# Another list of attention steps in a fused attention and two-stage mixture-of-experts kernel

## The chip, the core and the metric

The kernel runs on one core of one Trainium2 chip. The time is device microseconds of one execution; three executions of the kernel before gave 986.51, 991.4 and 991.65 us, median 991.4. All other times here come from one profiled execution, whose own time is 991.88 us and whose span (first to last instruction) is 990.1 us.

## The reference, cut to what matters

Three layers follow each other. Attention with a block-causal mask works on 4 batches x 8 heads x 576 rows x 64 columns in f32; its output, as 2304 rows of 512, goes through a mixture of 8 experts with the two best experts of each row, and then through a second mixture with the one best expert of each row:

```python
scores = scale * np.matmul(q, k.transpose(0, 1, 3, 2))
scores = np.where(block_i >= block_j, scores, -1000000000.0)     # blocks of 64
attn = np.exp(scores - max) / (sum + 1e-09);  x = attn @ v
logits = x @ w_gate;  noisy = logits + log1p(exp(x @ w_noise)) * noise      # two best of 8
out[mask] += top2_w * (relu(x[mask] @ w1[e]) @ w2[e])
```

The second mixture has its own gate `w_gate2` (512 x 8) and its own weights.

## The kernel before, in words

Attention works on 16 pairs of heads. The work of a pair is cut into steps of two or three letters: TQ, TK and T4 transpose q, k and the last 64 rows on TensorE; QH, KH, A4 (ScalarE) and QL, KL, D4 (VectorE) split them into a high and a low part; S0, S1, S2, S8 are the score products; M and N the row maxima (VectorE), E the exponentials (ScalarE); B and BT transpose the exponentials, H and L split them; V0, V1, VX multiply with v, C copies, X0 and X1 multiply with an identity matrix beside the first gate's weights (IW), XC copies out.

TensorE, ScalarE and VectorE run in exactly the order in which the program issues the steps. That order is written out by hand in the string `ORDER` (lines 19 to 46 of the kernel), 1076 words. The n-th TK in it is that of pair n. Besides steps, there are three other words:

- `w3` puts three matmuls on a constant (L1161) into TensorE's queue.
- `a` takes one step of the routing of the first mixture.
- `h` takes the next entry of a list of side jobs ("heap") that is sorted by a time written beside each entry. There are 26 words `h`. The first four entries are `consts1` (small constants, eight noise loads nz, the triangle matrix tri on VectorE), `consts2` (more constants, the loads of wg2 = `w_gate2`, mid and bias1), the first part of `consts3`, and the load of the first quarter of expert weights; after them come zero fills of X1 and X2 in DRAM, three more quarters of weights and their splits.

```python
elif n == "h":
    heapq.heappop(heap)[2]()
...
for kk in range(4):
    ten.transpose(pt[:, kk], wg2[:, kk], ident)      # consts3, first part
act.activation(wt, pt.rearrange("e k d -> e (k d)"), AF.Copy)
```

So the first part of `consts3` puts four transposes of wg2 into TensorE's queue and a copy into ScalarE's, at the place of the third `h`.

GpSimd (POOL) and the queue that issues most loads and stores (SP) are not in the hand-written order; a scheduler places their instructions. Both still run one after the other: an instruction that waits holds all behind it. The loads of k and q for pair p+3 are issued when TQ, TK and T4 of pair p are; the step VS of pair p+2 (split of v on POOL) comes behind V0, V1 and VX of pair p, and the load of v for pair p+4 behind that. Lines: L906 and L911 are the loads of q, k, v; L200 and L201 the noise; L217 wg2; L218 mid; L226 the zero fills; L1147 and L1148 the stores of attention rows into X1; L472 the weights. L92 is a recording layer through which all compute instructions go.

After attention a part that is emitted by a clock model of the program runs both mixtures; nothing of it is touched.

Of the kernel before, what the change touches and what calls it, by code (L numbers as in the profile page):

```python
# [16 lines left out]
ET = mybir.EngineType  # L17

ORDER = """
TQ TK T4 h QH KH A4 h QL h KL w3 S1 h S2 TK TQ D4 M1 M2 E1 KH E2 QH T4 w1 S0 w2 S8 M0 KL M8 QL N8 A4 E0 w1 B5 w2 S1  # L20
B0 H5 E8 H0 D4 L5 M1 S2 B3 B2 E1 H3 H2 L0 M2 L3 L2 BT S8 VX B1 B4 HT E2 H1 H4 CX M8 LT N8 L1 L4 S0 TK TQ T4 V0 E8 KH
QH A4 C0 M0 KL QL h D4 R2 h BT S1 h V1 B3 B5 E0 HT H3 H5 M1 LT L3 L5 B0 S2 B2 B4 H0 C1 E1 H2 H4 L0 M2 L2 L4 VX h B1
h S0 TK TQ CX H1 E2 L1 M0 T4 V0 S8 KH QH A4 C0 E0 R2 KL D4 M8 QL N8 V1 S1 B0 h B1 X0 E8 H0 H1 C1 XC0 M1 L0 L1 S2 B3
B2 B4 E1 H3 H2 H4 M2 L3 L2 L4 S0 X1 B5 VX BT E2 XC1 H5 HT CX M0 L5 LT TK S8 V0 T4 TQ KH E0 C0 A4 QH KL M8 N8 R2 D4
QL B0 V1 B1 S2 X0 H0 H1 E8 C1 XC0 L0 L1 M2 BT B3 S1 X1 HT H3 E2 XC1 LT L3 R2 M1 B4 B2 S0 B5 VX H4 H2 E1 H5 CX L4 L2
L5 M0 X0 TQ h TK V0 S8 XC0 KH QH C0 E0 QL KL M8 N8 T4 B5 V1 S1 B0 A4 E8 C1 H5 H0 D4 M1 L5 L0 X1 S0 h BT B4 E1 XC1 HT
H4 M0 L4 LT B1 VX S2 B3 B2 H1 E0 H3 H2 CX L1 M2 L3 L2 X0 S8 TQ TK V0 E2 QH XC0 KH M8 N8 QL KL R2 C0 E8 h X1 T4 V1 B4
S1 A4 XC1 H4 C1 D4 h M1 L4 B3 B0 S2 BT H3 H0 HT E1 L3 L0 LT M2 B2 B1 VX B5 S0 H2 H1 CX H5 E2 L2 L1 L5 M0 TK TQ V0 T4
S8 KH QH C0 E0 A4 QL KL M8 D4 R2 N8 V1 B0 B5 h S1 B1 H0 C1 H5 H1 E8 L0 L5 L1 M1 X1 XC1 TQ VX B3 BT S0 QH H3 HT E1 QL
L3 LT R2 M0 X0 B4 B2 S2 CX XC0 H4 H2 E0 L4 L2 h M2 X0 TK V0 T4 S8 KH XC0 C0 E2 A4 M8 KL N8 D4 V1 B5 B0 B2 S8 H5 H0  # L30
H2 E8 C1 L5 L0 L2 M8 N8 X1 BT B3 S1 XC1 HT H3 E8 LT M1 L3 B1 VX B4 S0 H1 H4 CX E1 L1 L4 R2 M0 TK TQ V0 S2 T4 QH KH
C0 E0 A4 QL KL M2 D4 V1 BT B0 S0 TQ HT H0 C1 E2 QH LT L0 M0 QL R2 X0 XC0 X1 h S2 X1 X0 XC1 E0 XC1 XC0 B2 B1 B4 S1 H2
H1 M2 L2 L1 H4 L4 M1 TK E2 KH a B3 VX KL H3 L3 S8 E1 B5 a H5 M8 L5 h CX TQ a a N8 QH QL a E8 S2 TK KH V0 T4 C0 A4 a
M2 a BT S1 V1 R2 a KL a D4 a E2 B5 HT B3 M1 H5 S8 a LT a B0 h L5 B2 a H3 E1 L3 H0 S0 B4 a M8 a C1 L0 a H2 L2 B1 VX a
H4 L4 X0 a H1 CX L1 TQ XC0 a TK N8 QH E8 a M0 a V0 QL T4 S2 a KH C0 KL V1 B5 a A4 E0 D4 a H5 a M2 B1 S8 a a H1 L5 E2
a B0 L1 H0 a X0 C1 a h S0 a M8 a XC0 N8 L0 a E8 B4 R2 B3 B2 a H4 M0 a L4 a H3 L3 a VX S1 H2 E0 X1 BT HT L2 a T4 M1
S0 A4 a LT a D4 a CX M0 a a a V0 E1 XC1 C0 S8 B4 a a R2 E0 V1 B0 a M8 a a H4 H0 a N8 E8 a X0 L4 L0 S1 a XC0 B1 H1 a
TQ QH L1 BT QL HT a LT M1 C1 a S2 B2 TK H2 KH a L2 X1 a VX E1 KL B5 XC1 M2 a H5 L5 a X1 B3 a S1 E2 H3 L3 M1 a S0 XC1
T4 a TQ CX A4 E1 D4 a TK M0 V0 QH QL a C0 S8 a KH E0 B1 M8 KL V1 B3 a S2 H1 H3 B5 R2 L1 N8 H5 E8 C1 L3 L5 a X0 XC0 h
a B4 B0 S2 X1 a H4 a M2 H0 a L4 a E2 XC1 L0 B2 VX H2 M2 a BT T4 S0 CX HT L2 TK a h h LT V0 A4 a E2 D4 a TQ KH B5 a  # L40
M0 C0 QH a a S1 a KL QL a E0 a a V1 B0 a H5 B3 H0 a M1 S8 a a L5 H3 a X0 E1 L0 BT a M8 L3 R2 N8 a C1 S2 B4 XC0 a HT
LT E8 H4 M2 VX a B2 B1 L4 H2 L2 S0 CX a H1 L1 a X1 E2 a T4 a M0 a V0 A4 XC1 a C0 a a D4 E0 a a BT S1 V1 M1 a h B5 S8
a HT a LT a a E1 H5 a C1 a a B0 H0 a JT0 M8 JH0 L5 JT1 N8 X0 a JH1 L0 a h R2 X1 B1 XC0 a JL0 JL1 a E8 VX B2 H1 XC1 a
a a JM0 CX a B3 a H2 L1 R2 B4 JM1 a a a a L2 JR0 a H4 JV0 a JM2 L4 a a H3 L3 a V0 JS0 JR1 C0 JR2 JV1 JM3 B0 a a V1
B2 JM4 BT JM5 JV2 a JR3 JS1 H0 H2 HT JV3 a L0 L2 LT JR4 JR5 a JV4 JV5 a h a C1 a B5 a VX B3 B1 JM6 a H5 a L5 a B4
JM7 JS2 H3 CX H1 H4 JR6 a L3 a L1 L4 JR7 a JV6 a X1 JV7 V0 JS3 X0 XC1 a C0 V1 X0 XC0 C1 XC0 X1 a XC1
"""


# [1643 lines left out]
```

## Time and profile before

| | us |
|---|---|
| median of three executions | 991.4 |
| the profiled execution's own time | 991.88 |
| its span | 990.1 |
| TensorE busy | 925.7 |
| VectorE, GpSimd, ScalarE busy | 676.0, 506.9, 465.1 |

The page cuts the span into 40 slices of 24.75 us with the busy share of each engine in tenths. A view of stretches gives the busy time of each engine between two times. The timeline gives instructions with start, duration, names and, in square brackets, how long the engine had stood idle before and what ended that. The view of waits sums up these by engine and by what was waited for.

### The profile page before, as it was taken

Reading aid. Unit: us, or ns where it says so; the run is one execution under the profiler, and the core shown is the slowest. Engines: PE = TensorE matmul, PEld = TensorE weight load, DVE = VectorE, ACT = ScalarE, POOL = GpSimd, SP = SyncE. Lnnn points to the kernel's source line nnn. Section 1 sums busy time; section 2 is a strip of 40 time slices with the busy share of each in tenths; the row PEclk is TensorE's granted clock in tenths of the full one; section 3 lists DMA queues with packets and bytes.
Section 4 is the critical chain, followed back from the end, with each engine's and each line's share of the span. In section 5 each row is a group of like instructions: output and inputs, shape, how many; then the busy total and the mean of one; then the engine's idle time right before and its main releaser. Section 6 shows DMA issues by size and latency. Waiting matters only on the chain. (4 is left out here: it accounts for less than half of the span.)

```text
span 990.1 us, 16259 instructions
## 1 busy us (share of the span) xinstructions
PE 925.7 (93%) x5655; PEld 807.8 (82%) x5655; DVE 676.0 (68%) x1639; ACT 465.1 (47%) x1026; POOL 506.9 (51%) x585
## 2 busy tenths in 40 slices
PE   2599999999889988999999999999999999999995
PEld 1378888878879877998989899897988878888895
DVE  1497888988838789839487593979859686233241
ACT  1498989877644143433333333333333333343352
POOL 3044455385231665968486684847966226222122
PEclk7799999999999999999999999999999999999998
DMA  6784433223158545747365463734646446443440
GB/s 128 215 257 118 120 92 93 66 80 81 34 170 269 107 92 144 160 126 144 94 146 111 127 130 88 143 95 86 151 126 128 123 139 191 139 128 107 138 130 13
DMA packets 145292, 124.49 MB, mean 126 GB/s; under 512 B 75625, under 2 KB 115945, under 8 KB 145074
## 3 DMA queue, kind: packets, MB, share of 16 engines
q1 hardware_dynamic: 126242, 90.14, 31.4%
q0 software_dynamic: 17904, 32.96, 17.0%
q8 instruction: 47, 0.77, 0.3%
q10 hardware_dynamic: 1056, 0.26, 0.1%
q14 instruction: 43, 0.35, 0.1%
HBM read 95.50 MB, written 28.09 MB: 125 GB/s over the span
## 5 line engine op out<-in xcount | busy, mean ns | idle before, releaser
L92 POOL TENSOR_TENSOR wl<-raw,wh 128x1024 fp32r<-128x1024 f32 (+1 forms) x91 | 189.4, 2128 | 97.8 <-ACT wh L92 95.3
L92 DVE SCALAR_TENSOR_TENSOR zero<-py,gts,wide 128x512 f32<-128x512 f32 x296 | 221.6, 749 | 8.2
L92 PE MATMUL ph<-xth,wh 128*128 128x312 f32 (+4 forms) x672 | 217.1, 323 | 4.3 <-DVE kp L92 3.4
L92 PE MATMUL ph<-xtl,wh 128*128 128x312 f32 (+4 forms) x672 | 216.8, 323 | 0.4 <-DVE xtl L92 0.4
L92 PE MATMUL ph<-xth,wl 128*128 128x312 f32 (+4 forms) x672 | 217.0, 323 | 0.0
L92 PE MATMUL py<-wh,kp 128*128 128x512 f32 x488 | 165.2, 399 | 3.7 <-DVE zero L92 3.7
L92 PEld LDWEIGHTS ph<-xth,wh 128*128 128x128 f32 x672 | 127.6, 190 | 10.0 <-DVE kp L92 3.7
L92 PEld LDWEIGHTS ph<-xtl,wh 128*128 128x128 f32 x672 | 127.4, 190 | 5.8 <-DVE xtl L92 0.6
L92 PEld LDWEIGHTS ph<-xth,wl 128*128 128x128 f32 x672 | 127.0, 189 | 5.1
L92 ACT ACTIVATE wh<-raw 128x1024 fp32r<-128x1024 f32 x112 | 117.8, 1052 | 4.6 <-DMA raw<-in_moe_w_dram 4.6
L92 ACT ACTIVATE yr<-py,gts 128x512 f32<-128x512 f32 x59 | 40.6, 689 | 152.1 <-PE py L92 103.4
L92 PEld LDWEIGHTS py<-wh,kp 128*128 128x128 f32 x488 | 92.4, 189 | 23.3 <-DVE zero L92 4.4
L92 PE MATMUL py<-wl,kp 128*128 128x512 f32 x244 | 95.9, 393 | 0.0
L92 DVE SCALAR_TENSOR_TENSOR hl<-ph,hh 128x312 fp32r<-128x312 f32 (+5 forms) x84 | 43.0, 512 | 76.0 <-ACT hh L92 74.5
L92 PE MATMUL py<-wh,hh 128*128 128x512 f32 x228 | 92.8, 407 | 0.0
L92 PE MATMUL py<-wh,hl 128*128 128x512 f32 x228 | 89.7, 393 | 0.0
L92 PE MATMUL py<-wl,hh 128*128 128x512 f32 x228 | 89.5, 393 | 0.0
L92 POOL DMA_INDIRECT X<-yr,ids x40 | 63.4, 1585 | 44.6 <-ACT yr L92 25.8
L92 POOL DMA_INDIRECT xr<-X,ids x54 | 54.9, 1017 | 61.0 <-PE px L92 46.5
L92 ACT ACTIVATE hh<-ph 128x312 fp32r<-128x312 f32 (+5 forms) x84 | 38.3, 456 | 101.8 <-PE ph L92 98.2
L92 ACT ACTIVATE p<-ps,nm 128x384 f32<-128x384 f32 (+4 forms) x160 | 82.2, 532 | 6.5 <-DVE nm L92 5.6
L92 DVE TENSOR_TENSOR wl<-raw,wh 128x1024 fp32r<-128x1024 f32 x42 | 56.9, 1357 | 35.4 <-ACT wh L92 35.3
(277 smaller groups left out, 1724.6 us busy)
## 6 DMA issues: line engine op xcount, KB each, us to landing
raw<-in_moe_w_dram SPq DMA_DIRECT2D x112, 512.0 KB
X<-zero SPq DMA_DIRECT2D x13, 512.0 KB
kld<-in_k_dram SPq DMA_DIRECT2D x32, 128.0 KB
vld<-in_v_dram SPq DMA_DIRECT2D x32, 128.0 KB
X<-x SPq DMA_DIRECT2D x16, 256.0 KB
qld<-in_q_dram SPq DMA_DIRECT2D x30, 128.0 KB
wide<-in_moe_w_dram SPq DMA_DIRECT2D x4, 512.0 KB
wide<-WG2T POOLq DMA_DIRECT2D x1, 2048.0 KB
```

Source lines behind the costliest of these rows:

```text
L92: return f(*a, **kw)
```

## The change

The string `ORDER` is replaced by another one with the same 1076 words, each as often as before. The steps of a pair stand in much the same sequence. The words `h` stand elsewhere: as words number 3, 7, 9, 13, 85, 88, 91 ... (counted from 0) in the list before, and as words number 72, 176, 185, 204, 207, 220 ... in the new one. The entries that they take are the same, in the same sequence.

```diff
 ORDER = """
-TQ TK T4 h QH KH A4 h QL h KL w3 S1 h S2 TK TQ D4 M1 M2 E1 KH E2 QH T4 w1 S0 w2 S8 M0 KL M8 QL N8 A4 E0 w1 B5 w2 S1
...
+TQ TK T4 QH KH A4 QL KL w3 S1 S2 TK TQ D4 M1 M2 E1 QH E2 KH w1 S0 T4 w1 S8 M0 KL QL M8 N8 A4 E0 w2 B5 w2 B0 S1 H5 E8
...
```

On TensorE, behind the transposes of pair 0 (kld is k, tld the last rows, ident an identity matrix, wg_80 is wg2) and ahead of the three matmuls of `w3` on the constant `ones`. The row with a minus stands there in the list before only:

```order
 L92 MATMUL pt<-ident,kld 128x128 x4
 L92 MATMUL pt<-ident,tld 128x128
-L92 MATMUL pt<-ident,wg_80 8x128 x4
 L1161 LDWEIGHTS ones
 L1161 MATMUL pa<-ones 128x512
```

The four transposes of wg2 are gone from there. In the new kernel TensorE has them far behind, between S8 of pair 3 and V1 of pair 2 (kh, kl, kp are the parts of k and q; PTh those of the exponentials, vs those of v):

```order
L92 MATMUL ps<-kh,kp_156 128x288
L92 MATMUL ps<-kl,kp_156 128x288
L92 MATMUL ps<-kh,kp_158 128x288
L92 MATMUL pt<-ident,wg_80 8x128 x4
L92 MATMUL pa<-PTh,vs 128x448 x2
L92 MATMUL pa<-PTh,vs 128x320
```

In SP's queue, before, the loads of pair 3 (kld, qld) are followed by the eight of the noise, wg2, mid and bias, then the first weights (wide) and zero fills, and then pair 4; the last of these rows are:

```order
L201 DMA nz<-in_moe_noise_dram 64x8
L217 DMA wg_80<-in_moe_w_gate_dram 128x4x8
L218 DMA mid<-in_moe_modality_id_dram 128x36
L220 DMA bias_91<-in_moe_modality_bias_dram 1x16
L472 DMA wide<-in_moe_w_dram 128x4x256
L247 DMA LG<-zero 128x207
L226 DMA X_60<-zero 128x2x512
L234 DMA WG2T<-wide 8x512
L226 DMA X_60<-zero 128x3x512
L906 DMA tld<-in_q_dram 64x2x64
```

Now the loads of pair 4 stand ahead of the noise, those of pair 5 and v of pair 4 (vld) between the noise and wg2:

```order
L201 DMA nz<-in_moe_noise_dram 64x8
L906 DMA tld<-in_q_dram 64x2x64
L906 DMA tld<-in_k_dram 64x2x64
L911 DMA kld<-in_k_dram 128x4x64 x2
L911 DMA qld<-in_q_dram 128x4x64 x2
L906 DMA vld<-in_v_dram 64x2x64 x2
L911 DMA vld<-in_v_dram 128x4x64 x2
L217 DMA wg_80<-in_moe_w_gate_dram 128x4x8
L218 DMA mid<-in_moe_modality_id_dram 128x36
```

So wg2's load moved back by pair 4's and pair 5's loads and by a load of v that itself waits for POOL.

## Rows read from the trace of the kernel before

**Rows 1.** The page: 40 slices of the span, busy tenths of TensorE and its granted clock.
```profile
PE   2599999999889988999999999999999999999995
PEclk7799999999999999999999999999999999999998
```
**Rows 2.** Waits, first 60 us: us in total, times, longest.
```profile
PE pt L92 <- DMA wg<-in_moe_w_gate_dram: 26.1, 1, 26.1
```
**Rows 3.** Timeline of TensorE at the start: start, us, engine, line, instruction.
```profile
1.42 3.60 PE L1161 MATMUL pa<-ones 128*128 128x512 bf16 x8 [1.42 <-DVE ones L1156]
...
7.13 0.27 PE L92 MATMUL pt<-ident,tld 128*128 128x128 f32 x1
33.53 1.01 PE L92 MATMUL pt<-ident,wg 128*8 128x128 f32 x4 [26.13 <-DMA wg<-in_moe_w_gate_dram]
34.34 1.49 PE L1161 MATMUL pa<-ones 128*128 128x512 bf16 x3
35.75 0.58 PE L92 MATMUL ps<-kh,kp 64*128 64x256 f32 x2
...
37.86 0.66 PE L92 MATMUL pt<-ident,kld 128*128 128x128 f32 x4
```
**Rows 4.** Timeline of SP's queue: times of issue, not of landing.
```profile
5.69 1.06 SPq L911 DMA_DIRECT2D qld<-in_q_dram  x2
...
25.58 1.06 SPq L911 DMA_DIRECT2D qld<-in_q_dram  x2
26.69 0.51 SPq L200 DMA_DIRECT2D nz<-in_moe_noise_dram  x1
...
31.36 0.59 SPq L217 DMA_DIRECT2D wg<-in_moe_w_gate_dram  x1
...
39.09 0.63 SPq L906 DMA_DIRECT2D tld<-in_q_dram  x1
```
**Rows 5.** Timeline of VectorE at the start.
```profile
2.63 0.60 DVE L92 TENSOR_SCALAR tri<-jp 128x128 bf16<-128x128 f32 x1
...
7.96 0.69 DVE L92 TENSOR_TENSOR kl<-pt,kh 128x512 fp32r<-128x512 f32 x1
```
**Rows 6.** Timeline of ScalarE at the start.
```profile
34.58 0.59 ACT L92 ACTIVATE wide<-pt 8x512 f32<-8x512 f32 x1 [26.13 <-PE pt L92]
```
**Rows 7.** Stretches: length, busy us (instructions) by engine, then granted clock, DMA share, GB/s.
```profile
8.75:35.75 27.00, 2.22 (x7) 0.81 (x7) 0.41 (x3) 0.59 (x1) 6.05 (x14) 0.53 0.55 110
35.75:250.00 214.25, 203.87 (x1607) 174.71 (x1606) 187.46 (x447) 186.22 (x573) 106.12 (x258) 0.98 0.45 125
250.00:300.00 50.00, 44.00 (x310) 40.36 (x311) 31.34 (x85) 25.20 (x56) 15.12 (x34) 0.97 0.40 113
35.75:60.00 24.25, 22.10 (x161) 16.66 (x160) 20.84 (x47) 20.53 (x66) 5.10 (x13) 0.96 0.91 309
```
**Rows 8.** Stretches of 1 us: the granted clock is the third number from the end.
```profile
36.00:37.00 1.00, 1.00 (x10) 0.90 (x12) 0.14 (x1) 0.00 (x0) 0.00 (x0) 0.50 1.08 396
38.00:39.00 1.00, 1.00 (x10) 0.89 (x9) 0.93 (x2) 1.00 (x5) 0.00 (x0) 1.00 1.04 406
202.00:203.00 1.00, 1.00 (x7) 0.79 (x6) 1.00 (x3) 0.86 (x3) 1.00 (x2) 0.50 0.19 42
```
**Rows 9.** Timeline of TensorE later.
```profile
43.40 0.59 PE L1161 MATMUL pa<-ones 128*128 128x512 bf16 x2
...
77.27 0.60 PE L92 MATMUL pt<-ident,kld 128*128 128x128 f32 x4
...
200.37 0.66 PE L92 MATMUL pt<-ident,p 128*128 128x128 f32 x4 [1.90 <-DVE PTl L92]
...
296.92 1.00 PE L92 MATMUL px<-ident,wide 128*128 128x128 f32 x4 [4.50 <-DVE xtl L92]
```
**Rows 10.** Timeline of POOL: the split of v of pair 2.
```profile
59.34 2.14 POOL L92 TENSOR_TENSOR vs<-vld,vs 128x128 fp32r<-128x128 f32 x5
```
**Rows 11.** Waits of SP's queue over the whole span.
```profile
SPq L1147 <- POOL x L92: 57.9, 12, 16.5
```

More of the change, by code (lines that the diff above doesn't have):

```diff
@@ L19 @@
 ORDER = """
-TQ TK T4 h QH KH A4 h QL h KL w3 S1 h S2 TK TQ D4 M1 M2 E1 KH E2 QH T4 w1 S0 w2 S8 M0 KL M8 QL N8 A4 E0 w1 B5 w2 S1
[L21 to L44, printed above, removed]
@@ L45 @@
-B2 JM4 BT JM5 JV2 a JR3 JS1 H0 H2 HT JV3 a L0 L2 LT JR4 JR5 a JV4 JV5 a h a C1 a B5 a VX B3 B1 JM6 a H5 a L5 a B4
-JM7 JS2 H3 CX H1 H4 JR6 a L3 a L1 L4 JR7 a JV6 a X1 JV7 V0 JS3 X0 XC1 a C0 V1 X0 XC0 C1 XC0 X1 a XC1
+TQ TK T4 QH KH A4 QL KL w3 S1 S2 TK TQ D4 M1 M2 E1 QH E2 KH w1 S0 T4 w1 S8 M0 KL QL M8 N8 A4 E0 w2 B5 w2 B0 S1 H5 E8
+D4 L5 M1 B2 B3 S2 H0 H2 E1 H3 L0 L2 M2 L3 BT B4 S8 VX B1 H4 HT E2 H1 CX LT M8 L4 L1 N8 TK S0 T4 V0 h TQ KH A4 E8 C0
+QH KL R2 M0 QL D4 B3 V1 S1 E0 H3 M1 L3 B0 B5 S2 BT C1 H0 H5 HT E1 L0 L5 LT M2 B2 VX B4 B1 S0 H2 H4 CX H1 E2 L2 L4 L1
@@ new lines @@
+M0 TQ TK V0 T4 S8 KH QH A4 C0 E0 QL KL M8 D4 R2 N8 X0 V1 B1 B0 S1 E8 H1 H0 XC0 C1 L1 L0 M1 S2 B2 B3 B4 VX H2 H3 H4
+E1 L2 L3 L4 M2 X1 BT B5 S0 XC1 HT H5 CX E2 LT L5 M0 TK TQ T4 V0 h S8 KH A4 QH C0 E0 D4 QL h M8 KL R2 N8 V1 B0 B1 X0
+S2 H0 H1 E8 C1 XC0 L0 L1 M2 S1 h BT B3 h X1 HT H3 E2 XC1 LT L3 M1 B4 VX B5 B2 h S0 H4 H5 H2 CX E1 L4 L5 L2 M0 TQ TK
+h V0 h S8 X0 QH KH C0 E0 XC0 M8 QL N8 KL R2 V1 B0 T4 B5 S1 E8 H0 A4 C1 H5 L0 M1 D4 L5 S0 X1 B4 VX BT E1 XC1 H4 HT CX
+M0 L4 LT B1 h S8 B3 B2 H1 E0 H3 H2 L1 M8 N8 L3 L2 X0 S2 TQ TK V0 XC0 E8 QH KH M2 QL KL E2 C0 X1 T4 B4 h V1 h S1 A4
@@ new lines @@
+XC1 H4 D4 R2 M1 L4 B0 B3 S2 BT H0 H3 C1 HT E1 L0 L3 LT M2 B1 VX B2 B5 S0 H1 CX H2 H5 E2 L1 L2 L5 R2 M0 TK TQ V0 T4
+S8 KH QH C0 E0 A4 KL M8 N8 QL D4 V1 B5 S1 B0 B1 E8 H5 H0 H1 M1 L5 L0 L1 S0 X1 C1 E1 XC1 B3 TQ VX BT S2 H3 QH HT M0 h
+L3 QL LT B4 B2 X0 E0 H4 H2 CX M2 L4 L2 S8 TK V0 T4 E2 XC0 KH C0 A4 KL M8 D4 R2 N8 X0 V1 B0 h B5 S8 E8 H0 XC0 H5 C1
+L0 M8 L5 N8 h B3 B2 S1 VX BT H3 H2 E8 HT L3 L2 LT M1 X1 B1 B4 h S0 XC1 H1 H4 CX E1 L1 L4 h M0 TK TQ T4 V0 S2 KH A4
+QH C0 E0 KL QL D4 h M2 V1 h BT TQ B0 S0 HT C1 QH H0 LT R2 QL L0 X1 B2 X0 E2 XC1 H2 XC0 M0 L2 B3 S1 X1 X0 H3 E0 XC1
@@ new lines @@
+XC0 L3 M1 R2 E1 S2 B1 TK H1 M2 L1 KH VX S8 KL M8 E2 TK a KH N8 a B5 H5 B4 a KL a S2 H4 CX TQ L5 QH a L4 T4 a V0 A4 a
+QL a E8 C0 a S1 a M2 a D4 a T4 A4 D4 a M1 a a E2 V1 B2 B0 H2 H0 L2 L0 X0 a S8 M8 a E1 B3 C1 XC0 N8 B1 a B4 H3 L3 H1
+S0 B5 H4 a L1 VX a BT E8 L4 H5 S2 a HT CX L5 a TQ LT V0 TK a R2 QH a M0 QL a C0 KH V1 a a a B4 KL B5 a E0 H4 a H5 X0
+a M2 L4 L5 a S8 E2 M8 a BT XC0 HT B0 LT S0 a H0 N8 a E8 B1 L0 a B3 M0 a C1 a B2 H1 H3 L1 S0 a a R2 a H2 E0 h L3 a VX
+X1 L2 a CX T4 S1 V0 A4 M0 a M1 a D4 a TQ a XC1 a C0 QH B2 a QL E0 a a V1 X0 H2 B4 L2 XC0 H4 L4 S8 BT TK E1 a a B0 a
@@ new lines @@
+M8 S2 a HT KH LT X1 H0 C1 a KL N8 E8 L0 B3 XC1 H3 R2 a M2 VX B1 L3 S1 H1 B5 L1 M1 a H5 L5 CX X1 V0 a T4 E2 a a XC1
+E1 a TK a a S0 S1 A4 D4 TQ KH C0 M0 QH KL QL E0 a B0 a M1 V1 X0 B1 S2 H0 L0 B3 H1 XC0 E1 H3 a L1 M2 L3 a C1 a E2 S8
+BT VX M8 B5 HT B2 a LT H5 N8 E8 a R2 S2 L5 X1 a B4 H2 a M2 S0 a XC1 L2 H4 L4 M0 T4 TK a CX h V0 TQ E2 a KH a A4 D4 a
+S1 KL a C0 QH E0 a V1 a BT B5 HT M1 QL S8 LT a H5 E1 B3 H3 L5 M8 B0 L3 C1 a S2 a H0 a N8 B2 H2 X1 L0 VX a L2 R2 B1 a
+E8 M2 CX a B4 XC1 H4 L4 H1 L1 S0 a a a E2 h X0 R2 a M0 a a T4 A4 V0 a D4 S1 a a a M1 a XC0 C0 E0 B0 a a a V1 B1 H0
@@ L47 @@
+S8 X0 L0 a H1 L1 M8 E1 JT0 C1 JT1 a XC0 a B5 a N8 JH0 JH1 E8 a JL0 a JL1 X1 H5 a a a L5 a a a B3 H3 a XC1 a VX JM0 a
+B4 H4 JR0 L3 L4 B2 JM1 H2 BT JM2 a JV0 a a a JR1 CX HT a JV1 JM3 JR2 a L2 a a LT BT JS0 V0 C0 a JR3 JM4 JR4 a V1 JM5
+B2 a JV2 R2 HT a JV3 B1 a a h JV4 LT a JR5 H2 H1 JV5 L2 h h L1 a B0 H0 JM6 JR6 a L0 JV6 B4 a C1 B5 B3 a VX a H4 a H5
+a h a L4 a H3 L5 a JM7 L3 CX JS1 a JS2 a X0 V0 JS3 h X1 a a C0 JR7 JV7 XC0 V1 C1 X0 X1 a XC0 XC1 XC1
 """
```

## The prediction, as it was put on record

> **What bounds the kernel now.** I read the page's slices first, then the waits, the timelines of the start, and the stretches. TensorE is busy nine tenths or more in nearly all slices; the exception at the front is two slices with 2 and 5 tenths, where its granted clock is also down to 7 tenths [rows 1]. So the kernel is bound by TensorE except in its first 40 us. The waits name one cause there: a single wait of 26.1 us for the load of wg2 [rows 2]. The timeline shows it in place: the last transpose of pair 0 starts at 7.13 and takes 0.27, so TensorE is through with it at 7.40; next in its queue are the four transposes of wg2, which start at 33.53; then the three matmuls of w3, and at 35.75 the first score product of the kernel [rows 3]. TensorE can't step past a waiting instruction, so all of attention stands behind a 512 x 8 matrix that attention does not use.
>
> Why the load is late is in SP's queue. It is issued at 31.36, behind the loads of pairs 0 to 3 (the last at 25.58) and eight loads of the noise, one about every 0.58 us from 26.69 on [rows 4]. From issue to the first transpose it takes 33.53 - 31.36 = 2.2 us [rows 3, 4]. VectorE had the low part of k of pair 0 ready at 7.96 + 0.69 = 8.65 [rows 5], the high parts before that. The stretch from 8.75 to 35.75 holds next to nothing: 2.22 us of TensorE, 0.41 of VectorE, 0.59 of ScalarE [rows 7].
>
> From 35.75 to 250 us TensorE is busy 203.87 of 214.25 us, VectorE 187.46, ScalarE 186.22; from 250 to 300 TensorE is busy 44.00 of 50 [rows 7]. Idle there are 10.4 + 6.0 = 16.4 us, in many short waits on VectorE and ScalarE, such as 1.90 at 200 and 4.50 at 297 [rows 9].
>
> **The change, part by part.** *The hole.* The transposes of wg2 leave the place behind pair 0. TensorE is through with pair 0 at 7.40, and w3 follows at once; in the trace the first score product starts 35.75 - 34.34 = 1.41 us after w3 does, so now at 7.40 + 1.41 = 8.81 [rows 3]. The second factor it needs is there at 8.65 [rows 5]. The first score product moves from 35.75 to 8.81: 26.9 us.
>
> *What would be late next.* Pair 1's transposes come 37.86 - 35.75 = 2.1 us after it [rows 3], at 10.9; its q and k are issued by 5.69 + 1.06 = 6.8 us in both kernels [rows 4], and 2.2 us later they are there. Pair 3's are issued by 25.58 + 1.06 = 26.6 [rows 4] and needed more than 27 us after the first score product. Pair 4's loads wait for TensorE's transposes of pair 1 and therefore for the hole: 39.09 [rows 4]. Now nothing holds them, and they go at 26.7; pair 4's transposes ran at 77.27 [rows 9] and will at about 50.4. They have 20 us of room. I count nothing for loads.
>
> *The clock.* The score products at 36 to 37 run at 0.50 of the clock, that is 1.2 GHz, since TensorE had stood still for 26 us; from 38 on it is 1.00, 2.4 GHz [rows 8]. Without the hole there is no such fall. S1 and S2 of pair 0 take 2.1 us [rows 3]; at the full level they take at least half of that, so the gain lies between 0 and 1.05 us. I take 0.5.
>
> For this the trace says two things. The granted clock is put at full for the first microseconds, but eight matmuls on the constant take 3.60 us at 1.42, or 0.45 each, and two of the same kind take 0.59 at 43.40, where the clock is full [rows 3, 9]. The Trainium skill (TensorE: Matmul & The Clock Gate, section What's actually happening) says that the throttled level is the default and activity releases it. The durations agree with the page, not with the column. By the page the first steps could still run at 1.2 GHz, the gain would be 0 and the sum 0.5 us longer.
>
> *What comes into busy time.* What ran in or ahead of the hole now stands among the steps of pairs 2 to 5. TensorE: the four wg2 transposes, start to start 34.34 - 33.53 = 0.81 at half clock [rows 3], so 0.4 at full. ScalarE: the copy, 0.59 [rows 6]. VectorE: the triangle matrix, 0.60 [rows 5]. From 35.75 to 60 those two are busy 20.53 and 20.84 of 24.25 us [rows 7], so cover is thin. The two act side by side, so at most 0.4 + 0.6 + 0.6 = 1.6, at least 0.4; I take 0.4 + 0.6 = 1.0.
>
> *New waits.* wg2's load now stands in SP's queue behind pair 4's loads (3.6 us: six issues of about 0.6), the noise (31.36 - 26.69 = 4.7), pair 5's (3.6), and v of pair 4 (2.4), which waits for POOL's split of pair 2. That split ends at 59.34 + 2.14 = 61.5 [rows 10], 34.6 on the new clock. From 26.7 this adds up to 41.0, and wg2 is there at 41.0 + 2.2 = 43.2. Its transposes stand behind pair 4's transposes, V0 of pair 2 and S8 of pair 3, so after 50.4: at least 7 us of room. POOL's copy of mid, which came right behind wg2 in SP's queue, now stands between the splits of pairs 2 and 3 on POOL. It lands about 44, so POOL stands there for 9 us. Behind it are only copies of the row sums for pair 1 and the split of pair 3, whose first reader is V0 of pair 3, beyond the transposes of pair 4. Cost 0; if the cover were gone, some 4 us.
>
> The zero fills, which came early and close together in SP's queue, are spread now; up to 60 us TensorE was busy 22.10 of 24.25 us at a DMA share of 0.91 [rows 7], so I count nothing for them either way.
>
> *The rest of the list.* The steps keep their counts and nearly their places. What the other order does to the 16.4 us of idle time, and to the falls of the clock behind some of them (0.50 at 202) [rows 8], cannot be read from a trace of the old order. From below: all of it goes, -16; from above: it doubles, +16. No row favours either end; I take 0 and keep some 8 to each side for the range, since half the idle time would have to change for more.
>
> **Sum.** 991.88 - 26.9 - 0.5 + 1.0 = 965.4. The profiled execution is 0.5 above the median of the runs shown, so 965.0.
>
> **The rivals.**
> (1) *The gap was used.* In the hole the loads and fills had the DMA engines to themselves: share 0.55 of 27.0 us [rows 7], 14.9 us of transfers. If these came to stand in front of TensorE later, 965.0 + 14.9 = 980. For it: the share is 0.91 in the next 24 us. Against it: TensorE's idle time there is only 2.15 us, and loads have the room worked out above.
> (2) *The steady part is better ordered.* Half of the 16.4 us of idle time goes: 965.0 - 8.2 = 957. For it: VectorE and ScalarE wait for order as much as for work; against it: the sequence of steps is nearly the same.
> (3) *The hole opens elsewhere.* If another instruction held the first score product as long, the time would be that of before less the clock, 991. Against: its inputs are all ready at 8.65.
> (4) *Slower: SP's queue held by stores.* In the new order, stores of attention rows, which wait for POOL, stand ahead of the loads of the pairs from 7 on, with zero fills between them. SP has stood behind such stores for 57.9 us in all, 16.5 at the longest [rows 11], and that did no harm since a pair's loads are issued far ahead (pair 4: 39.09 against 77.27) [rows 4, 9]. Where holds use up that room, TensorE waits for k and q, and the time lost comes in full: from 27 us on the kernel is slower, half of 57.9 gives 965.0 + 29 = 994. It decides when several holds in a row pass 30 us; one alone does not.
>
> **Chances.** My forecast, 965, with its own range 958 to 973: 0.70. Rival 1: 0.13. Rival 2: 0.12. Rival 3: 0.03. Rival 4: 0.02. The range for 8 in 10 takes rival 2's 957 and most of rival 1: 955 to 978. A difference of 0.5%, 5 us, is about what a measurement can tell from none. Faster by more: the forecast and rivals 1 and 2, 0.95; the same: rival 3, 0.03; slower: 0.02.
>
> **What would show it.** In the profile after: the wait for wg2 is gone from the list of waits; the first score product starts at 8.8 (between 8.6 and 10); the first slice has about 9 tenths from its second half on; from there to the end of attention it takes as long as before, within 8 us; wg2's transposes run near 55 with no wait in front; POOL stands for mid for some 9 us and nobody waits for it. Wrong would be: the score products of pair 1, 2 or 3 waiting for loads (rival 1), TensorE idle for kld or qld past 100 us (rival 4), or a start that is right while the part up to 300 us is longer or shorter by over 8 us, which no row here could tell.

## The result, and the profile after

The kernel with the new list takes 956.92 us (median of 4 executions, 952.34 to 964.91), the kernel before 991.52: ratio 0.9671, 95% interval 0.9599 to 0.9743. That is 34.6 us less; 26 were forecast. The time lies inside the range for 8 in 10 (955 to 978) and just below the forecast's own range (958 to 973). The profiled execution is the fastest of the four, 952.34 us with a span of 950.6.

The page of the new kernel, slices of the span, answers to [rows 1]. The two weak slices at the front are gone and TensorE's granted clock has no fall there:

```profile
PE   8999989999899899999999999999999999999995
PEclk9999999999999999999999999999999999999998
```

The start of TensorE's timeline in the new kernel (start, us, engine, line, instruction, in brackets the idle time before it and what ended that) answers to [rows 3]:

```profile
7.09 0.27 PE L92 MATMUL pt<-ident,tld 128*128 128x128 f32 x1
7.20 0.81 PE L1161 MATMUL pa<-ones 128*128 128x512 bf16 x3
7.94 0.39 PE L92 MATMUL ps<-kh,kp 64*128 64x256 f32 x2
8.66 0.38 PE L92 MATMUL ps<-kl,kp 64*128 64x256 f32 x2 [0.34 <-DVE kl L92]
...
9.79 0.66 PE L92 MATMUL pt<-ident,kld 128*128 128x128 f32 x4
...
50.49 0.60 PE L92 MATMUL pt<-ident,wg 128*8 128x128 f32 x4
```

The first score product starts at 7.94 instead of 35.75, 27.8 us earlier. The transposes of wg2 stand at 50.49 with no wait in brackets: between wg2's issue and them lie 7.4 us, as SP's queue in the new kernel shows (answers to [rows 4]):

```profile
31.43 0.51 SPq L200 DMA_DIRECT2D nz<-in_moe_noise_dram  x1
...
43.07 0.51 SPq L217 DMA_DIRECT2D wg<-in_moe_w_gate_dram  x1
```

The list of waits of the first 60 us in the new kernel (us in total, times, longest) has no wait for wg2 any more, which [rows 2] showed. The longest is one of POOL:

```profile
POOL midf L92 <- DMA mid<-in_moe_modality_id_dram: 14.9, 1, 14.9
```

Four stretches of the new kernel (length, busy us and instructions of PE, PEld, DVE, ACT, POOL, then granted clock, DMA share, GB/s), the last two as long as the second and third of [rows 7], both 27 us earlier:

```profile
8.75:35.75 27.00, 25.77 (x198) 19.88 (x199) 24.12 (x57) 24.18 (x78) 9.99 (x25) 1.00 0.58 117
35.75:60.00 24.25, 23.83 (x195) 21.38 (x194) 18.65 (x43) 21.74 (x69) 11.96 (x35) 1.00 0.72 194
...
8.75:223.00 214.25, 207.21 (x1677) 180.01 (x1678) 187.95 (x468) 190.50 (x586) 114.97 (x284) 1.00 0.53 140
223.00:273.00 50.00, 45.10 (x295) 40.69 (x295) 32.98 (x83) 25.05 (x49) 14.64 (x24) 0.97 0.52 158
```

Idle in the last two rows are 7.0 + 4.9 = 11.9 us, where [rows 7] gave 16.4. The column of the granted clock shows 1.00 from the start to 256 us; in the kernel before, it fell at 201 and at 235 in the part that corresponds, besides the hole.

Three landmarks say where the profiled executions come apart: the first score product, the first transpose of the last stage of attention (`ps<-ident,wide`) and the first matmul of the mixture (`py<-wh,kp`). First the rows of the kernel before, then those of the new one; the last row of before is a wait inside the mixture:

```profile
248.33 0.66 PE L92 MATMUL ps<-ident,wide 128*128 128x128 f32 x4
...
282.90 0.48 PE L92 MATMUL py<-wh,kp 128*128 128x512 f32 x1
...
378.15 0.43 PE L92 MATMUL ph<-xth,wh 128*128 128x368 f32 x1 [3.42 <-DVE kp L92]
```
```profile
214.72 1.07 PE L92 MATMUL ps<-ident,wide 128*128 128x128 f32 x8
...
246.67 0.47 PE L92 MATMUL py<-wh,kp 128*128 128x512 f32 x1
```

The first score product is 27.8 us earlier, the last stage 33.6, the mixture 36.2. Behind that, the two differ by another 3.3 us, about as much as the wait for kp, which the new kernel has not; of the four kernels with all steps old below, two have it in their profiled execution and two lack it. So the start gave what was forecast, and the steps between the first score and the mixture gave 8.4 us on top in this execution, the fastest of four; in the second profile of the same kernel, below, they gave 5.3.

### The profile page after: what moved, and what is told of

Its sections match the earlier page's. It is cut to its first block, busy times and chain, and to the rows that moved or that the text cites. A ratio compares the mean times of both kernels' runs of the same rounds, so it can differ in the third digit from the quotient of the medians.

```text
span 950.6 us, 16262 instructions
## 1 busy us (share of the span) xinstructions
PE 919.9 (97%) x5655; PEld 804.4 (85%) x5655; DVE 665.0 (70%) x1639; ACT 463.7 (49%) x1026; POOL 508.5 (53%) x585
## 5 line engine op out<-in xcount | busy, mean ns | idle before, releaser
L92 ACT ACTIVATE kp<-ph 128x312 fp32r<-128x312 f32 (+5 forms) x84 | 38.4, 457 | 91.2 <-PE ph L92 83.5
```

The source lines that it names most:

```text
L92: return f(*a, **kw)
```

## The experiments

Two questions were open: is it the places of the words `h` or the order of the steps, and what else of the old list stood behind the wait for wg2. In all kernels below the count of every word is that of before. "Before" beside each is the kernel before on the same chip.

**Old steps, side jobs at the new places.** The 26 words `h` of the old list at the new list's numbers, the other words as they were.

```diff
-TQ TK T4 h QH KH A4 h QL h KL w3 S1 h S2 TK TQ D4 M1 ...
+TQ TK T4 QH KH A4 QL KL w3 S1 S2 TK TQ D4 M1 ...
```

> The steps in the order of before, but every side job (word h) at the word number it has in the new list. The hole at the start is gone in this kernel as in the new one. Theory A (only the places of the side jobs count, the order of the other steps is worth nothing): as the new kernel, 957 within 4. Theory B (the hole is worth 27 us and the other order of the steps the remaining 7): 964 within 3. In both the first score product starts near 8 us.

Measured: 974.02 us (before 987.35), ratio 0.9861 [0.9839, 0.9883]. Neither expectation holds. The trace shows a loss that belongs to no theory: the first score product starts at 7.5, but at 126 us TensorE stands still and runs at half clock afterwards. First the row of TensorE, then that of VectorE, then a stretch of 1 us (the granted clock is the third number from the end):

```profile
129.75 1.09 PE L92 MATMUL pt<-ident,qld 128*128 128x128 f32 x4 [3.22 <-issue]
```
```profile
126.14 1.55 DVE L92 TENSOR_TENSOR wl<-wide,wh 128x512 fp32r<-128x512 f32 x2 [2.90 <-DMA tld<-in_k_dram]
```
```profile
141.00:142.00 1.00, 1.00 (x7) 1.00 (x6) 0.00 (x0) 0.53 (x2) 0.25 (x1) 0.50 0.00 0
```

The split of the fourth quarter of weights (wl) stands in VectorE's queue at word 471 and starts late. The row puts the wait down to a load, but the split reads wh, which ScalarE had ready at 126.1 without having waited for data. The row maxima and the splits of k for the next pairs stand behind the split. TensorE is granted 0.50 from 129 to about 142.

**The same, with that one split (and the zero fill behind it) back at its old word.**

```diff
-... A4 QL KL h M2 D4 h V1 BT B0 S0 TQ HT ...       (words 471, 474)
+... A4 QL KL M2 D4 V1 ...                           (h at words 491 and 527)
```

> The old list's steps with all words h at the new list's numbers (974.0), but the fourth split back at word 491 and the fill behind it at 527, as in the list before. Theory: the wait of 3.2 us at 126.5 and the half clock from 129 to 142 behind it come from that one word, 3.2 + about 6 us, so 965. Rival: the steps themselves are the worse ones and the loss moves on, 972 to 974.

Measured: 962.23 us (before 987.87), 0.9741 [0.9714, 0.9769]. The time is a little below the 965 expected. The two words cost 974.02 - 962.23 = 11.8 us. In the profiles 9.0 of it lie between 114 and 184 us of the run above, where the wait of 3.2 and the half clock behind it stand; 2.4 lie in the mixture, where the run above has the wait for kp and this one has not. So the old steps without the hole and without that collision give 25.6 us; the forecast without any gain of the steps was 26.4.

**New list, the first three side jobs back at words 3, 7 and 9.**

```diff
-TQ TK T4 QH KH A4 QL KL w3 S1 S2 ...
+TQ TK T4 h QH KH A4 h QL h KL w3 S1 S2 ...
```

> The new list with the first three side jobs only (small constants, the load of the second gate's weights, their transposes) back at words 3, 7 and 9. Theories A and B: the wait of 26 us for that load is back and TensorE starts its first score product near 35 us; 957 + 27 = 984. Rival (the hole was covered by loads that the kernel has to wait for anyway): under 975.

Measured: 986.36 us (979.89 to 991.77, 10 executions; before 987.35), 0.9969 [0.9944, 0.9995], near the 984 of theories A and B: the hole is back, and next to nothing is left of the gain. TensorE's timeline of this kernel:

```profile
33.54 1.01 PE L92 MATMUL pt<-ident,wg 128*8 128x128 f32 x4 [26.91 <-DMA wg<-in_moe_w_gate_dram]
...
35.76 0.58 PE L92 MATMUL ps<-kh,kp 64*128 64x256 f32 x2
...
151.28 2.19 PE L92 MATMUL pt<-IW,oT 128*128 128x80 f32 x10 [2.03 <-DVE PTh L92]
```

This takes 29.9 us away from the new list's 956.5 (measured again, below). Between the profiles it is 984.5 - 950.6 = 33.9 us of span: 27.8 by the first score product and 6.1 behind the last row, where a wait of 2.03 us is followed by 14 us at 0.50 of the clock. The new list has the same wait at the same instruction (2.04 us at 123.42, shown below) without a fall of the clock.

**Old list, only wg2's load moved.** It is issued right behind the load of k of pair 0.

```diff
             load(0, "k")
+            nc.sync.dma_start(wg2, w_gate2.rearrange("(k p) e -> p k e", p=128))
```

> The kernel before with one edit: the load of the second gate's weights is issued right behind the first loads of k instead of with the other constants; its transposes stay where they were, ahead of the first score product. If the wait for that load is the whole of the hole: first score product at 9 to 10 us, time 991.5 - 26 = 965, and what the new list has beyond that (8 us) is not here. If the transposes and the copy behind them cost something at this place: 966 to 968. Rival (other loads follow up and hold TensorE, since pair 1's come 0.6 us later): above 970.

Measured: 971.32 us (before 987.35), 0.9851 [0.9818, 0.9884]. The first score product starts at 9.08, and yet 16 us are gained, not 26. The number is the rival's (above 970), but not its reason: TensorE waits for no load of pair 1. It waits again, for the next small load in line, bias1, which the old list has at its words 7 and 85; at 38 us the clock is still at half:

```profile
34.71 0.57 PE L92 MATMUL pt<-bias,one 1*128 1x16 f32 x2 [8.12 <-DMA bias<-n_moe_modality_bias_dram]
```
```profile
38.00:39.00 1.00, 1.00 (x5) 0.96 (x5) 0.28 (x1) 1.00 (x4) 0.00 (x0) 0.50 0.98 222
```

**Old list, wg2's and bias1's loads moved.** As above, with the load of bias1 behind that of wg2.

> The list before, with the loads of wg2 and of bias1 (the two that TensorE was seen to wait for in turn) issued right behind the load of k of pair 0; nothing else is changed. Theory: after the wait for wg2 only the wait for bias1 (8.1 us) and the stretch at half clock behind it (about 11 us, worth some 4) are left in the start, so 971.3 - 8.1 - 4 = 959, with the first score product near 9 and the first transposes of the last stage near 219. Rival: something else in the old list is late next, and the time stays at 966 or above.

Measured: 974.18 us (971.73 to 977.47, 6 executions, the profiled one the slowest; before 987.87), 0.9848 [0.9819, 0.9878]. The theory fell, the rival was right: a third wait takes the place of the second. The list of waits from 20 to 45 us in this kernel:

```profile
PE pt L92 <- DVE PTh L92: 10.3, 1, 10.3
DVE wl L92 <- ACT wh L92: 10.2, 1, 10.2
ACT wh L92 <- DMA wide<-in_moe_w_dram: 9.8, 1, 9.8
```

Read upwards it is one chain: the first quarter of weights is issued on SP at 33.90 behind the noise and mid, ScalarE stands for it, VectorE for ScalarE, TensorE for VectorE. The old list calls for this split at word 91, which comes up near 27 us in a start without a hole; in the kernel before, VectorE does the same split at 55.81. So three side jobs stood where they did no harm behind a start that was 27 us late, and taking one wait away shows the next.

**The new list once more.**

> The new kernel itself, unchanged, for a second profile and more times beside the others: 957, runs from 952 to 965 as seen. If the runs differ by several us, a second profile shows in which stretch: theory (waits of TensorE in attention's second half, where routing shares VectorE) puts it between 100 and 260 us; rival (weights' splits in the mixtures) behind 300 us.

Measured: 956.5 us (954.54 to 964.06, 6 executions; before 987.35), 0.9704 [0.9671, 0.9736]. That is 30.9 us less, against 17 executions of the kernel before. Its trace differs from the first one of the same kernel: the second quarter of weights is issued at 75.24 instead of 73.88 and lands late for its split. ScalarE's, then TensorE's row, then a stretch:

```profile
81.61 1.06 ACT L92 ACTIVATE wh<-wide 128x1024 fp32r<-128x1024 f32 x1 [2.09 <-DMA wide<-in_moe_w_dram]
```
```profile
83.63 0.66 PE L92 MATMUL pt<-ident,p 128*128 128x128 f32 x4 [1.53 <-ACT xu L92]
```
```profile
85.00:86.00 1.00, 1.00 (x6) 0.67 (x6) 1.00 (x2) 0.16 (x1) 1.00 (x3) 0.50 0.99 272
```

From 76 to 91 us this execution lost about 3 us on the other one, and 1.7 more in the mixture. The larger part lies where neither expectation had put it (100 to 260, or behind 300).

**New list, two splits later.** The second split from word 306 to 330, the fourth from 471 to 497, with the `h` behind each.

```diff
-... KL E2 C0 X1 T4 B4 h V1 h S1 A4 ...       (words 306, 308; 471, 474)
+... KL E2 C0 X1 T4 B4 V1 S1 A4 ...           (330, 332; 497, 498)
```

> The new list with two of the four splits of weight quarters later: the second from word 306 to 330 (the fetch behind it from 308 to 332), the fourth from 471 to 497 (the zero fill behind it from 474 to 498). Theory: the median of the new kernel, 956.5, and its spread (952 to 965) come from splits that stand on ScalarE and VectorE before their data has landed, with a fall of TensorE's clock behind; with room for the landing 953, within 951 to 955 in all runs. Rival: the split costs its own time wherever it stands, 956.5, with the same spread.

Measured: 951.55 us (950.54 to 955.28, 6 executions; before 987.87), 0.9636 [0.9607, 0.9665], wholly below the interval of the new list in the run above. The time came as expected. The spread shrank, from 9.5 us in the run above to 4.7, but two of the six lie outside the expected 951 to 955. The reason given, data that has not landed, holds for one of the two splits only. In the second profile of the new list the second split waits for its data (2.09 us at 81.61 above); the fourth does so in neither profile. ScalarE computes its high part right behind exponentials, with no wait in brackets (first profile):

```profile
119.00 1.08 ACT L92 ACTIVATE wh<-wide 128x1024 fp32r<-128x1024 f32 x1
```

VectorE stands 2.01 us for that (second row of the next experiment). So the fourth split collides with the order of ScalarE's steps, not with its load.

**New list, the low parts of the weights on POOL.**

```diff
-                at(50 + 14 * i + 11, lambda: stage.split(vec))
+                at(50 + 14 * i + 11, lambda: stage.split(gps))
```

> The new list, with the low parts of the four weight quarters computed by POOL (GpSimd) instead of VectorE. VectorE's order holds TensorE, POOL's does so less: theory 952 to 954 (four times 1.5 us of VectorE gone, about half of it on the path). Rival: POOL holds the splits of v or the stores longer, and the time is the same or longer, 957 to 962.

Measured: 950.55 us (before 987.87), 0.9623 [0.9593, 0.9653], a little below the expected 952 to 954. One split takes POOL 2.53 us where VectorE took 1.56 (rows of this kernel's POOL and of the new kernel's VectorE), and from the first score product to 250 us no wait of TensorE above 0.8 us is left; in the new kernel the third row below stood behind the split:

```profile
80.25 2.53 POOL L92 TENSOR_TENSOR wl<-wide,wh 128x512 fp32r<-128x512 f32 x2 [1.06 <-ACT wh L92]
```
```profile
120.11 1.56 DVE L92 TENSOR_TENSOR wl<-wide,wh 128x512 fp32r<-128x512 f32 x2 [2.01 <-ACT wh L92]
```
```profile
123.42 1.34 PE L92 MATMUL pt<-IW,oT 128*128 128x80 f32 x10 [2.04 <-DVE PTh L92]
```

**Both.** Later splits, and on POOL.

> The new list with the two later splits and with the low parts of all four splits on POOL. Each alone gave 951.6 and 950.6 where the new list gives 956.5. Theory: both take away the same thing (a split that stands on VectorE while TensorE waits behind it), so together they give little more than one, 949.5 to 951. Rival: they add up, 951.6 - 5.9 = 945.7.

Measured: 953.19 us (before 988.6), 0.9651 [0.9628, 0.9675]. That is above the expected 949.5 to 951 and far from the rival's 945.7. They don't add up: in the trace of each alone the wait of 2.04 us at 123.42 is gone already. The three are not told apart by their intervals; all beat the kernel before, and the intervals of the first two lie below that of the new list (0.9671 to 0.9736).

**Half of the steps new, half old.** With the side jobs at the words of the later splits: the first 500 steps from one list, the rest in the order of the other.

> Side jobs at the words of the kernel with the later splits (951.6). The first 500 steps in the new list's order, the others in the old list's order. Between the kernel with later splits and the one with the old steps and the late fourth split (962.2) the first transposes of pair 10 are 4.1 us apart, the first matmul of the mixture 10.4. Theory: the gain of the new order of steps is spread, some 4 us ahead of pair 10 and some 6 behind, so this one loses the second part: 951.6 + 6 = 958. Rival: it all comes from one side, 951.6 or 962.

> The counterpart: side jobs at the same words, the first 500 steps in the old list's order, the others in the new list's. Theory: it loses the first part, 951.6 + 4 = 956. Rival: it all comes from one side, 962 or 951.6.

Measured: 960.63 (0.9722 [0.9699, 0.9745]) with the new half first, 960.26 (0.9720 [0.9697, 0.9744]) with the old half first; before 988.6; expected were 958 and 956. Each loses about 9 us, together 18, where the whole difference is 10.7. The halves don't add up. Probably a cut at 500, where the lists have issued different steps, costs something of its own; that isn't shown, and this pair can't say which half is worth what.

**Only the last 228 steps old.** The cut is at 822, where the lists have issued the same steps but one.

> Side jobs at the words of the kernel with the later splits (951.6). The first 822 steps in the new list's order, the other 227 in the old list's; at this word the two lists have issued the same steps but one, so there is next to no seam. Theory: the waits of TensorE that every run with the old steps shows from there on (1.55 for PTl and half clock behind it, 1.40 for kh, 0.91 for kp) come back, and the first matmul of the mixture starts some 3.6 us later than in the kernel with later splits (10.4 us lead there, 6.8 at the transposes of pair 15): 955. Rival: those waits belong to the whole old order, and this part alone is worth nothing, 951.6; or the cost of a seam, which the two halves showed (about 9 us each), comes here too, 960.

Measured: 959.29 us (956.07 to 959.64; before 987.53), 0.9708 [0.9688, 0.9729]. The waits that the old steps have at this place come back one by one. TensorE's timeline of the kernel before, of the old steps with new side jobs (the second experiment), and of this one:

```profile
234.04 1.34 PE L92 MATMUL pt<-IW,oT 128*128 128x80 f32 x10 [1.55 <-DVE PTl L92]
...
250.38 0.66 PE L92 MATMUL ps<-ident,wide 128*128 128x128 f32 x4 [1.39 <-ACT kh L92]
...
262.65 0.39 PE L92 MATMUL ps<-kh,wh 128*128 128x256 f32 x1 [0.91 <-ACT kp L92]
```
```profile
208.68 1.34 PE L92 MATMUL pt<-IW,oT 128*128 128x80 f32 x10 [1.56 <-DVE PTl L92]
...
223.48 0.66 PE L92 MATMUL ps<-ident,wide 128*128 128x128 f32 x4 [1.40 <-ACT kh L92]
...
235.77 0.39 PE L92 MATMUL ps<-kh,wh 128*128 128x256 f32 x1 [0.91 <-ACT kp L92]
```
```profile
202.93 1.34 PE L92 MATMUL pt<-IW,oT 128*128 128x80 f32 x10 [1.57 <-DVE PTl L92]
...
217.72 0.66 PE L92 MATMUL ps<-ident,wide 128*128 128x128 f32 x4 [1.40 <-ACT kh L92]
...
230.00 0.39 PE L92 MATMUL ps<-kh,wh 128*128 128x256 f32 x1 [0.91 <-ACT kp L92]
```

The new list has neither of the first two, and 0.52 us of the third. From first score product to first matmul of the mixture the trace has 242.1 us, against 238.3 with all steps new: 3.8, as expected (3.6). The median does not settle it: it is 7.7 above that kernel's, nearer to the rival of a seam (960) than to 955; the profiled execution, the fastest of five, is 4.9 above.

For the last stage all traces together do. From its first transpose to the first matmul of the mixture it takes 34.5 or 34.6 us in all seven profiles that have it in the old order, and 31.9 or 32.0 in all seven that have it in the new one, whatever stands ahead of it and wherever the side jobs stand. The wait of 1.4 for kh is in each of the first seven and in none of the others; the one for kp is 0.91 us there and 0.52 here. So 2.6 us of the gain are shown to belong to the order of the steps there. For the steps ahead of it, and for some 3 us of this run's median, the size stays open.

## Why the prediction was right, and where it was short

*The sum.* The forecast counted 26.4 us for the hole and what goes with it, and nothing for the order of the steps. The old steps without the hole and without the collision gave 25.6, so that part was right. The time that came, 957, is rival 2's, to which I had given 0.12. How much lies beyond the forecast depends on the executions: 34.6 us were gained in the first measurement, 30.9 in the second. The sum started from an execution of 991.88 us with the wait of 3.42 us in the mixture; on the other chips the kernel before has medians of 987 to 989. No term had that; which execution the sum starts from is luck. (991.88 - 26.9 - 0.5 + 1.0 is 965.5 and not 965.4; the 965.0 stands.)

*The hole.* Right. 27.8 us against 26.9. The step was a little off in its own terms: it added 1.41 us from `w3` to the first score product, which was a distance at half clock; at full clock it is 7.94 - 7.20 = 0.74. That is why the start lies below the band of 8.6 to 10. The first product needs only the high parts; it is the second one, at 8.66, that waits 0.34 us for the low part kl, as the 8.65 of [rows 5] says.

*The clock.* Right in size, with the doubt settled. The three matmuls of `w3` take 0.81 us, 0.27 each, where [rows 3] had 0.45 each for the first eight at 1.42: the engine is at its upper level by 7.2. The first two products take 0.39 instead of 0.58, and S1 and S2 of pair 0 take 9.79 - 7.94 - 0.34 = 1.5 us instead of 2.1. So 0.6 against 0.5 taken, and the lower case, in which the first steps still ran at 1.2 GHz, did not come.

*What would be late next.* Right for the new list: no wait of TensorE above 0.5 us between the first score product and 120 us in the profiled execution. The reason given, that inputs of pairs 1 to 4 are early enough, was only half of it. The experiments with one and two loads moved show that in the old list two more side jobs were late next, bias1 (8.1 us) and the first split of weights (10.3). The new list gains by having moved those too; I had followed only wg2. Removing the named wait by itself was worth 16 us.

*What comes into busy time.* Not separable. Its bound of 1.6 us lies below what the runs can tell.

*New waits.* wg2: right, with 7.4 us from issue to use. It was issued at 43.07, not at 41.0. POOL stands for mid for 14.9 us and not 9, and nobody waits for it: right in effect, wrong in size.

*Zero fills, and rival 1, that the gap was used.* From 35.75 to 60 us TensorE's idle time fell to 0.42 us at a DMA share of 0.72. Rival 1's 980 came in no execution; the longest took 964.91. A small loss of its kind does show in the second profile: the late landing at 81.61 above, some 3 us.

*The rest of the list.* This is the step that was mis-sized. I took 0 with 8 to either side, on the ground that the sequence was nearly the same; it was -8.4 in the first profile, rival 2's amount, and -5.3 in the second. With over 8 us the first even met the last of the signs of being wrong that the prediction names. Idle time and clock both take part. The second experiment (old steps, side jobs out of the way) and the one with later splits (new steps) show it from the first score product to the mixture; besides the steps they differ in the words of two splits, a fetch and a fill. For each, the last stage of attention and the sum over that whole part:

```profile
221.40:256.00 34.60, 32.08 (x262) 30.83 (x261) 26.48 (x73) 20.85 (x50) 9.84 (x25) 1.00 0.19 59
sum 248.80, PE 234.09 PEld 203.68 DVE 212.50 ACT 205.93 POOL 120.04; mean PE 39.02 PEld 33.95 DVE 35.42 ACT 34.32 POOL 20.01
```
```profile
213.60:245.60 32.00, 31.01 (x259) 30.01 (x256) 26.12 (x75) 19.27 (x48) 9.41 (x20) 1.00 0.20 59
sum 238.40, PE 230.88 PEld 202.88 DVE 208.78 ACT 204.94 POOL 118.69; mean PE 38.48 PEld 33.81 DVE 34.80 ACT 34.16 POOL 19.78
```

Idle are 248.80 - 234.09 = 14.7 us in the old order and 7.5 in the new; 7.2 of the 10.4 us are idle time. The three waits above are 3.9 of it in the old order and 0.5 in the new one. Those, and a fourth in [rows 9] (1.90 at 200), could have been found in the trace of before and looked for one by one in the new list; I didn't. The other 3.2 are busy time, part of it the half clock behind such a wait. Against the new list itself, whose fourth split collides (2.04 us at 123.42), the old steps are 962.23 to 956.5, with intervals that overlap: the times alone do not show a gain of the steps there.

*Rivals 3 and 4.* Neither came: the first score product stood free, and TensorE never stood for kld or qld past 100 us in the new kernel.

## What to carry to other kernels

When one long wait heads a hand-placed order, list everything that the order put behind it by that late clock: each later job that had been placed to suit the hole becomes a wait of its own once the hole is gone, and moving one load gave 16 us, moving nearly all side jobs gave 26. Where an order of steps is replaced, go through the short waits of the old trace (1 to 2 us each) and look in the new order whether the two instructions still stand in that sequence: here idle time was 7 of the 10 us between the old steps and the new ones. A job that only has to be done some time belongs on an engine that holds nobody, or far enough behind its load that a late landing is covered, and at a place where no other engine has to do its part of the job first.

## What was not expected of the hardware

A short wait of TensorE can cost several times itself, and not always. With half the steps old, the wait of 1.55 us for PTl was followed by 4 us at 0.50 of the clock; with only the last steps old, the same wait at the same place (1.57) was followed by none. After 3.22 us without work (old steps, side jobs at the new places) TensorE ran at 0.50 for some 13 us; with the wait that cost 9.0 us. After 2.03 (new list, three side jobs back) it ran so for 14 us, at a cost of 6.1, and after the 2.04 at 123.42 in the new kernel, the same instruction, not at all. Stretches from the kernels with 2.03 us and 1.55 us of wait, the granted clock third from the end:

```profile
164.00:165.00 1.00, 1.00 (x6) 0.84 (x5) 0.56 (x2) 0.11 (x2) 1.00 (x4) 0.50 0.00 0
```
```profile
207.00:208.00 1.00, 1.00 (x5) 0.58 (x5) 0.97 (x6) 0.80 (x3) 0.15 (x1) 0.50 0.00 0
```

TensorE is busy for the whole of both stretches, and at its lower level all the same. What decides whether and how long it stays there the runs don't show.
